# Reordering the opening of two spectral layers on one core: channel-matrix splits and cell sums moved behind the first blocks

## Chip, core and metric

The kernel runs on one NeuronCore of a Trainium2 chip. The metric is the device time of one execution in microseconds (us). The profile gives the granted TensorE clock as a share of full speed.

## What is computed

Four layers in turn on a sequence of 2048 rows of 640 numbers, all float32: attention with a dilated window of 8, a Fourier mixing layer, and both again.

```python
x = A_x
x = x + _A_ref(_layernorm(x, axis=-1), A_wqkv, A_wo)
x = x + _B_ref(_layernorm(x, axis=-1), B_dft_seq_re, B_dft_seq_im, B_dft_hid_re, B_dft_hid_im)
x = x + _A_ref(_layernorm(x, axis=-1), A_wqkv, A_wo)
x = x + _B_ref(_layernorm(x, axis=-1), B_dft_seq_re, B_dft_seq_im, B_dft_hid_re, B_dft_hid_im)
...
def _B_ref(x, dft_seq_re, dft_seq_im, dft_hid_re, dft_hid_im):
    a = jnp.einsum("bsd,ed->bse", x, dft_hid_re)
    b = jnp.einsum("bsd,ed->bse", x, dft_hid_im)
    y = jnp.einsum("ts,bse->bte", dft_seq_re, a) - jnp.einsum("ts,bse->bte", dft_seq_im, b)
    return y
```

The change lies in the two `_B_ref` layers, called spectral layers here.

## The kernel before

Each float32 operand of a matmul is split into a high and a low part (`split`, line 127: a cast on ScalarE, then a subtraction on VectorE), and each product is made of three passes (high by high, high by low, low by high).

A spectral layer (`LayerB`, line 845) first multiplies by the sequence matrix, then by the channel matrices. Its 2048 output rows are 8 tiles of 256. For a tile the sequence matrix comes in 16 blocks of 256 KB.

- Tile 0's sums `z` are accumulated in five banks (`ZTAGS`: m0, m1, xt, t0, t1) while the attention layer before it still runs.
- `run` (line 1229) then takes over. `evac` (line 980) evicts tile 0's five banks as split parts (`zt_put`, lines 973, 975, 978). `load_w` loads and splits the two channel matrices in 10 pieces of 128 rows (`split`, lines 128, 130, 132).
- The loop over the 16 blocks of tile 1 follows: `zpart` (line 950) loads a block (line 944, five buffers `win`), splits it (lines 890 and 903, two buffers) and does 15 matmuls into the same five banks (line 918).
- Tile 0's products with the channel matrices, `ymm` (line 985, matmuls on line 996), stand in that loop: one for the first 128 rows, one for the second. `yout` (line 1004) adds the residual (line 1009), stores, and in the first spectral layer computes the statistics of the next layer norm (lines 148 and 150).
- The loop also issues the cell sums. The six other tiles are computed in three pairs, each by a scheme with seven products (`pair`, line 1093), for which sums of quarters of the input are needed. `x_whole` (line 1041) makes 8 sums of high and low parts, `x_combine` makes 20 sums or differences of cells (line 1049), splits them (lines 1050 and 1051, two buffers `stg`) and stores 512 KB each (line 1052). `pair` loads them back (line 1058) with its own blocks (line 1068), which it combines (line 1114) and splits (lines 1078, 1079) ahead of its matmuls (line 1085).
- At the end of `run` tile 1's banks are evicted; the first pair uses the same banks.

The layer norm of the last quarter of the rows (lines 868, 880, 881) ends just ahead of `run`. In `run` only TensorE's order is written by hand (`manual_schedule(engines={nc.tensor.engine})`); the framework's scheduler places the instructions of VectorE, ScalarE, GpSimd and the DMA queue on SyncE, each of which is then worked off in order.

The loop before:

```python
self.evac(0)
self.load_w()
...
for s in range(NST):
    self.zpart(1, s, s + 1)
    if s == 3:
        self.ymm(0, 0, 0, KD)
        self.yout(0, 0, nstats)
    if s == 13:
        self.ymm(0, 1, 0, 2)
    if s > 1:
        for fn, args in todo[:3]:
            fn(*args)
        todo = todo[3:]
```

Of the kernel before, what the change touches and what calls it, by code (L numbers as in the profile page):

```python
# [20 lines left out]
D = 640  # L21
# [15 lines left out]
LEAD0 = (-7, -6, -5, -4, -3, -2, -1, 0, 1, 1, 2, 3, 3, 4, 5, 5)  # L37


THIN = ((20, 24, 26, 28, 32, 36, 40, 44), (12, 16, 20, 24, 28, 32, 36, 44, 48))  # L40
OUTP = (((20, 24, 28, 32), (36, 40, 44, 46)), ((20, 24, 28, 32), (36, 40, 44, 46)))
LNS = ((40, 52), (40, 52))


LEAD2 = (-7, -6, -5, -4, -2, 0, 0, 1, 1, 2, 3, 4, 4, 6, 6, 7)
ZTHIRDS = (
# [4 lines left out]
)  # L51
# [3 lines left out]
NWIN = 5  # L55
# [19 lines left out]
def tile_layers(ctx: ExitStack, tc: tile.TileContext, x, wqkv, wo, cs, wre, wim, out):  # L75
# [21 lines left out]
    nc.vector.memset(warm, 0.0)  # L97
    nc.scalar.activation(warm, warm, AF.Exp)
    T([P, 8], "pad0")
# [34 lines left out]
    class Stats:  # L134
        def __init__(self):
# [30 lines left out]
        def var_eps(self, j):  # L166
            nc.scalar.activation(self.rstd[:, j : j + 1], self.var[:, j : j + 1], AF.Copy, bias=EPS, scale=1.0 / D)  # L167

        def finish(self, j0=0, j1=4):
            r = self.rstd[:, j0:j1]  # L170
# [19 lines left out]
    def load_x(src, j, tag="xa"):  # L190
        xt = T([P, D], tag, bufs={"xa": 2}.get(tag, 1))
        nc.sync.dma_start(xt, src[:, j, :])
        return xt
# [45 lines left out]
    def layer_a(li, stats, handoff, prev):  # L239
        xin, xout = xs[li], xs[li + 1]  # L240
        first = li == 0
        ly = li // 2
        nstats = [None] * NC
# [7 lines left out]
        win = {}  # L251
        lgs = {}
# [18 lines left out]
        def x_stats(c, j, fast=False):  # L271
            if j == 0:
                stats[c] = Stats()
# [88 lines left out]
        def qkv_evac(g, cqj):  # L362
            c, q, j = cqj
            if j % 2 == 0:
                sgs[q] = T([P, 6, 2, FE], "stg", bufs=2)
# [21 lines left out]
        def q_load(u):  # L387
            c, e = u // NE, half(u, 0)[0]
            src = qb[c][e // 2]
            qs[u] = T([P, NJ, FE], "qs")  # L390
# [34 lines left out]
        def qk_mul(u, jp):  # L425
# [4 lines left out]
            nc.gpsimd.tensor_tensor(pv[:, :, 0:10], pv[:, :, 0:10], pv[:, :, 10:20], op=ALU.add)  # L430
            prq[(u, jp)] = pv

        def qk_red(u, jp):
            if jp == 0:
# [3 lines left out]
                prq.pop((u, jp))[:, :, 0:10],  # L438
# [75 lines left out]
        def wo_add(c, j, e0=0, e1=2):  # L514
            for e in range(e0, e1):
                if e == 0 and j == 0:
                    nstats[c] = Stats()
# [27 lines left out]
        def wq_split(q, k):  # L545
            split(wq[q][:, 0, k], wq[q][:, 1, k], wq[(q, k)], eng=nc.gpsimd if k % 2 else None)
# [23 lines left out]
        def early():  # L570
# [8 lines left out]
            def xt(j, part):  # L579
# [3 lines left out]

            prev.pair(
                NPAIR - 1,
                stats,
                {
                    2: lambda: (x_get(0), x_get(1)),
                    4: lambda: xt(0, 0),
                    5: lambda: (xt(0, 1), x_get(2)),  # L590
                    6: lambda: xt(1, 0),
                    7: lambda: (w0(), xt(1, 1), x_get(3)),
                    ("y", 1): lambda: xt(2, 0),
                    ("y", 2): lambda: xt(2, 1),
                    "end": lambda: (xt(3, 0), xt(3, 1)),
                },
# [11 lines left out]
        def prologue_first():  # L608
            wq_begin(0)
            for j, (k0, k1) in enumerate(((0, 3), (3, 5))):  # L610
                if j:
                    T([P, 16], "pad2")
# [47 lines left out]
            for i in range(KD):  # L660
                at(LEAD0[0] + 1 + i // 2, "misc", wq_split, 1, i)
                at(LEAD0[0] + 3 + i, "misc", wq_split, 2, i)
                at(LEAD0[0] + 5 + i, "misc", wq_split, 3, i)

        if not first:
# [10 lines left out]
        for k in range(KD):  # L676
# [7 lines left out]
        order += [  # L684
            (c, 2 * qh + i, 2 * jh + j)
            for c in range(1, NC)
            for qh in range(2)
            for jh in range(2)
            for i in range(2)
            for j in range(2)  # L690
        ]
        gs = list(LEAD0 if first else LEAD2)
        tx = {(0, j): -8 for j in range(NJ)}
        st = 4
        while len(gs) < NGRP:
            if st % 2 == 0 and len(tx) < NC * NJ:
                c, j = divmod(len(tx), NJ)
                used = [i for i, x in enumerate(order) if x[0] == c - 1 and x[2] == j]
                if used[-1] < len(gs) and gs[used[-1]] < st:
                    tx[(c, j)] = st  # L700
            cap = 0 if st < 6 else 2 if st % 2 == 0 and st not in THIN[ly] else 1
            for _ in range(max(0, cap - gs[:16].count(st))):
                if len(gs) < NGRP and len(gs) <= 16 + st and tx.get(order[len(gs)][::2], st) < st:
                    gs.append(st)
            st += 1
# [28 lines left out]
        for c in range(1, NC):  # L734
            for j in range(NJ):
                b = tx[(c, j)]
                at(b - 4, "dma", x_load, c, j)
                if first:
                    at(b - 3, "actl", x_stats, c, j)
                    at(b - 2, "fin", x_fin, c, j)  # L740
# [3 lines left out]
        for c in range(2):  # L744
            for j in range(NJ):
                a = OUTP[ly][c][j]
                tp(a, "o", c, j, 0, 2, "t1", 0, "s0" if (c, j) == (1, 3) else "ot")
                tp(a, "o", c, j, 2, 5, "t0")
                at(a + 1, "dmar", r_load, c, j, "xa" if (c, j) == (1, 3) else "xr")
# [569 lines left out]
```

## Time and profile before

| | us |
|---|---|
| runs | 1800.17, 1804.51, 1807.22 |
| median | 1804.51 |
| profiled execution | 1801.87 |
| its span, first to last instruction | 1800.0 |
| first spectral layer's opening, tile 1's blocks to the first pair | about 404 to 492 |
| the same in the second spectral layer | about 1295 to 1383 |

Rows of the timeline give start, duration, engine, line, operation and tiles, then in brackets the idle time of the engine ahead of the first instruction and what ended it. `PE` is TensorE's matmuls, `DVE` VectorE, `ACT` ScalarE, `SPq` the queue that issues DMAs. `out<-in` names tiles.

### The profile page before, as it was taken

What the parts mean: (1) busy time and instruction counts of PE and PEld (TensorE: products, weight loads), DVE (VectorE), ACT (ScalarE), POOL (GpSimd) and SP (SyncE); (2) the same over time, 40 slices, a digit from 0 to 9 for tenths busy, and PEclk for the clock granted to TensorE, in tenths of its full rate; (3) what the DMA queues carried; (4) which work ended last, traced back from release to release, by engine and by line L of the source; (5) the groups of instructions that cost most, each with busy time, mean ns of one, the idle gap of its engine ahead of it and who ended that gap; (6) DMA issues with size and microseconds to landing.
All of it is one profiled execution on the core that took longest, in us unless ns stands there. A gap on an engine that the chain in (4) does not pass through costs nothing.

```text
span 1800.0 us, 26493 instructions
## 1 busy us (share of the span) xinstructions
PE 1735.3 (96%) x8798; PEld 1506.4 (84%) x8798; DVE 1391.0 (77%) x2135; ACT 818.6 (45%) x1708; POOL 633.5 (35%) x591
## 2 busy tenths in 40 slices
PE   9999997989999999999999999998899999999999
PEld 6889896877788888888888899987787888888888
DVE  5899899987767767768739988899777676677673
ACT  5544644544445445445533334444434443443441
POOL 3799898960000000000008987889400000000000
PEclk9999999999999999999999999999999999999999
DMA  6776667648787887888737856687687876876861
GB/s 232 225 264 205 212 206 250 216 147 293 255 264 256 284 271 251 290 270 268 246 124 223 284 183 199 201 300 260 218 283 258 265 237 219 267 230 228 265 211 53
DMA packets 273994, 423.59 MB, mean 235 GB/s; under 512 B 22688, under 2 KB 153248, under 8 KB 273600
## 3 DMA queue, kind: packets, MB, share of 16 engines
q1 hardware_dynamic: 270656, 419.92, 71.7%
q10 hardware_dynamic: 3200, 1.97, 0.4%
q8 instruction: 70, 1.15, 0.3%
q14 instruction: 68, 0.56, 0.1%
HBM read 336.66 MB, written 85.14 MB: 234 GB/s over the span
## 4 chain that ended last, share of the span: by engine, by line
PE 63%; DVE 14%; DMA 11%; POOL 6%; ACT 3%; issue 2%; SPq 0%; DVEq 0%; ACTq 0%; POOLq 0%
PE m L359 16%; PE aux L996 12%; PE t L1085 9%; PE m L1085 9%; PE pq L1085 5%; PE xt L1085 4%; DMA xc<-stg 4%; PE aux L506 4%; DVE pr L428 2%; DMA win<-cs_in 2%; DVE pr L466 2%; POOL pr L481 2%; POOL pr L430 1%; POOL r L868 1%; DMA xa<-cs_in 1%
## 5 line engine op out<-in xcount | busy, mean ns | idle before, releaser
L359 PE MATMUL m<-r,s 128*128 128x480 f32 x1920 | 438.9, 383 | 6.2 <-ACT s L229 3.8
L359 PEld LDWEIGHTS m<-r,s 128*128 128x128 f32 x1920 | 358.1, 190 | 60.8 <-ACT s L229 5.5
L1078 ACT CAST r<-win 128x512 fp32r<-128x512 f32 x251 | 152.9, 620 | 175.3 <-DVE win L1114 86.9
L171 POOL TENSOR_TENSOR stats<-stats,mhalf 128x1 f32<-128x1 f32 (+1 forms) x40 | 29.1, 727 | 565.8 <-ACT stats L167 565.7
L996 PE MATMUL aux<-r2a,zo 128*128 128x320 f32 x768 | 226.0, 309 | 0.0
L481 POOL TENSOR_TENSOR pr<-pr 128x640 f32<-128x640 f32 x126 | 204.5, 1623 | 41.9 <-DVE pr L466 41.5
L428 DVE TENSOR_TENSOR pr<-pq,win 128x1280 f32<-128x1280 f32 x128 | 189.8, 1483 | 26.9 <-ACT pq L401 24.6
L996 PE MATMUL aux<-pr,zo 128*128 128x320 f32 x704 | 207.8, 309 | 0.0
L1079 DVE TENSOR_TENSOR r<-win,r 128x512 fp32r<-128x512 f32 x251 | 168.9, 687 | 45.7 <-ACT r L1078 43.5
L466 DVE TENSOR_TENSOR pr<-pq,win 128x1280 f32<-128x1280 f32 x128 | 190.8, 1491 | 4.5 <-DVE pq L461 0.2
L430 POOL TENSOR_TENSOR pr<-pr 128x640 f32<-128x640 f32 x128 | 183.5, 1434 | 19.8 <-DVE pr L428 17.0
L1085 PE MATMUL m<-r,r 128*128 128x512 f32 x594 | 151.7, 390 | 0.8 <-DVE r L1079 0.5
L996 PEld LDWEIGHTS aux<-r2a,zo 128*128 128x128 f32 x768 | 144.1, 188 | 1.9
L918 PE MATMUL m<-s,r 128*128 128x512 f32 x384 | 120.3, 401 | 18.1 <-DMA s<-c0b 7.1
L996 PEld LDWEIGHTS aux<-pr,zo 128*128 128x128 f32 x704 | 132.2, 188 | 2.0
L1085 PE MATMUL t<-r,r 128*128 128x512 f32 x495 | 132.6, 390 | 0.0
L1085 PEld LDWEIGHTS m<-r,r 128*128 128x128 f32 x594 | 111.2, 188 | 24.8 <-DVE r L1079 1.1
L918 PE MATMUL t<-s,r 128*128 128x512 f32 x384 | 117.4, 394 | 2.4 <-DVE ot L978 2.4
L482 POOL TENSOR_TENSOR pr<-pr 128x320 f32<-128x320 f32 x126 | 114.5, 909 | 9.9
L366 ACT COPY stg<-m 128x480 f32<-128x480 f32 x128 | 70.9, 556 | 100.4 <-PE m L359 88.1
L436 DVE TENSOR_REDUCE lg<-pr 128x64 f32<-128x640 f32 x128 | 104.0, 813 | 11.2 <-POOL pr L430 11.1
L1085 PEld LDWEIGHTS t<-r,r 128*128 128x128 f32 x495 | 92.9, 188 | 19.9
(270 smaller groups left out, 3231.8 us busy)
## 6 DMA issues: line engine op xcount, KB each, us to landing
win<-cs_in SPq DMA_DIRECT2D x358, 256.0 KB, 4.3
r<-xc SPq DMA_DIRECT2D x240, 256.0 KB, 4.5
win<-kvb SPq DMA_DIRECT2D x96, 440.0 KB, 4.7
xa<-cs_in SPq DMA_DIRECT2D x124, 256.0 KB, 4.3
win<-kvb SPq DMA_DIRECT2D x64, 360.0 KB, 5.1
xc<-stg SPq DMA_DIRECT2D x40, 512.0 KB, 3.7
kvb<-stg SPq DMA_DIRECT2D x60, 320.0 KB, 3.9
xr<-xs SPq DMA_DIRECT2D x40, 320.0 KB, 3.2
```

Source lines behind the costliest of these rows:

```text
L359: nc.tensor.matmul(mt[g][:, : 3 * F], st[:, a, k], wq[q][:, b, k], start=n == 0, stop=n == 14)
L428: nc.vector.tensor_tensor(pr, q, wview(u, jp, 0, [[1, FE]]), op=ALU.mult)
L430: nc.gpsimd.tensor_tensor(pv[:, :, 0:10], pv[:, :, 0:10], pv[:, :, 10:20], op=ALU.add)
L436: nc.vector.tensor_reduce(lgs[u][:, 2 * jp : 2 * jp + 2].rearrange("p j w h -> p (j w h)"), prq.pop((u, jp))[:, :, 0:10], axis=AX.X, op=AL ...
L466: nc.vector.tensor_tensor(pr.rearrange("p j w (h d) -> p j w h d", d=DH), lgs[u][:, 2 * jp : 2 * jp + 2].unsqueeze(4).to_broadcast([P, 2, ...
L481: g.tensor_tensor(pr[:, :, 0:4], pr[:, :, 0:4], pr[:, :, 4:8], op=ALU.add)
L482: g.tensor_tensor(pr[:, :, 0:2], pr[:, :, 0:2], pr[:, :, 2:4], op=ALU.add)
L918: self.last = nc.tensor.matmul(self.z[t][k], self.xn[c][:, a, j, k * P : (k + 1) * P], self.ct[s][:, b], start=s == 0 and i == 0, stop=s = ...
L996: self.last = nc.tensor.matmul(self.ym[e][:, :320], zt[(k, a, ri)][:, j2 * P : (j2 + 1) * P], w[:, e * 320 : (e + 1) * 320], start=(k, a, ...
L1078: nc.scalar.copy(hi, raw)
L1079: nc.vector.tensor_tensor(lo, raw, hi.bitcast(F32), op=ALU.subtract)
L1085: nc.tensor.matmul(bank, w(a, kb), hl[b], start=start and (a, b) == (0, 0), stop=stop and (a, b) == (1, 0),)
```

## The change

Most of the diff moves constants into a table `CFG` and reads them from there; the values that the attention layers get are those they had. In `run` the table's entries are the same for both spectral layers: `pre` is 0 for every block, `post` says how many items of the list `todo` follow each block, `y` after which block each fifth of tile 0's two products comes.

```diff
+ 'run': [{'pre': [0, 0, 0, 0, 0, 0, 0, 0, 0, 0, 0, 0, 0, 0, 0, 0],
+          'post': [0, 4, 4, 4, 3, 3, 3, 3, 3, 3, 3, 3, 3, 3, 3, 3],
+          'y': [[6, 6, 6, 6, 6], [13, 13, 16, 16, 16]]},
...
+    eps = T([P, 1], "eps")
+    nc.vector.memset(eps, EPS)
+    nc.scalar.add_instruction(
+        mybir.InstLoadActFuncSet(name=nc.get_next_instruction_name(), ins=[], outs=[], act_func_set_id=6)
+    )
     nc.scalar.activation(warm, warm, AF.Exp)
-    T([P, 8], "pad0")
...
-        def load_w(self):
-            self.wr = T([P, 2, KD, D], "r2a", F32R)
-            self.wi = []
-            for k in range(KD):
-                raw = load_x(wre, k)
-                split(self.wr[:, 0, k], self.wr[:, 1, k], raw)
-                raw = load_x(wim, k)
...
+        def load_w(self, i):
+            k = i // 2
+            if i == 0:
+                self.wr = T([P, 2, KD, D], "r2a", F32R)
+                self.wi = []
+            if i % 2 == 0:
+                split(self.wr[:, 0, k], self.wr[:, 1, k], load_x(wre, k))
+            else:
+                wt = T([P, 2, D], f"pr{k}" if k < 4 else "zo3", F32R)
+                split(wt[:, 0], wt[:, 1], load_x(wim, k), neg=True)
+                self.wi.append((wt[:, 0], wt[:, 1]))
...
         def run(self, nstats):
+            R = CFG["run"][self.li // 2]
             self.evac(0)
-            self.load_w()
             todo = []
             for i in range(0, NP, 2):
                 todo += [(self.x_whole, (side, i)) for side in (2, 0)]
                 todo += [(self.x_combine, (m, i)) for m in XC]
+            todo = [(self.load_w, (i,)) for i in range(2 * KD)] + todo
             with tc.manual_schedule(engines={nc.tensor.engine}):
                 for s in range(NST):
+                    for _ in range(R["pre"][s]):
+                        fn, args = todo.pop(0)
+                        fn(*args)
                     self.zpart(1, s, s + 1)
-                    if s == 3:
-                        self.ymm(0, 0, 0, KD)
-                        self.yout(0, 0, nstats)
-                    if s == 13:
-                        self.ymm(0, 1, 0, 2)
-                    if s > 1:
-                        for fn, args in todo[:3]:
-                            fn(*args)
-                        todo = todo[3:]
+                    for h in range(2):
+                        ks = [k for k in range(KD) if R["y"][h][k] == s]
+                        if ks:
+                            self.ymm(0, h, ks[0], ks[-1] + 1)
+                        if 4 in ks:
+                            self.yout(0, h, nstats)
+                    for _ in range(R["post"][s]):
+                        if todo:
+                            fn, args = todo.pop(0)
+                            fn(*args)
```

So the code calls the 10 pieces of the channel matrices and the 28 cell-sum items behind blocks 1 to 12, and tile 0's first product comes behind block 6 in place of block 3. The number of matmuls and of DMAs is the same. The order of instructions in the two built programs:

- TensorE: the 60 matmuls of tile 0's first product stand behind block 6 in place of block 3, in both spectral layers; all else as before.
- GpSimd: as before.
- VectorE, ScalarE and the DMA queue: as before but for one memset at the start and a stretch in each spectral layer that begins with block 6. VectorE there, around the product's additions (line numbers of before; L1049 and L1051 belong to a cell sum, L903 to a block, L1041 to `x_whole`):

```
before, from block 6 to block 9:
  L1009 L1051 L1009 L1049 L1051 L903(6) L1049 L1051 L1049 L903(7) L1041 L1051 L1049 L903(8) L1041 L1051 L1049 L903(9)
after, from block 6 to block 9:
  L903(6) L1041 L1051 L130 L1049 L903(7) L1051 L903(8) L1049 L1051 L1049 L1051 L1049 L1009 L1041 L1051 L1009 L1049 L1041 L1051 L1049 L903(9)
before, around tile 1's eviction:
  L1049 L975 L1051 L1079 L1114 L1079 L1079 L978 L978 L975 L978 L1009 L1114 L1009 L978 L975
after, around tile 1's eviction:
  L1049 L975 L1079 L1051 L1114 L1079 L1049 L978 L978 L975 L1051 L1079 L1009 L978 L1009 L978 L975 L1079 L1114 L1114
```

More of the change, by code (lines that the diff above doesn't have):

```diff
@@ L54 @@
 STG = (-1, "dma2")
-NWIN = 5
+NWIN = CFG['nwin']
 ZTAGS = ("m0", "m1", "xt", "t0", "t1")
@@ L251, in layer_a @@
         win = {}
+        whole = {divmod(x, 2) for x in C["whole"]}
         lgs = {}
@@ L586, in early @@
                 stats,
[L587 to L596, printed above, removed]
+                {keys[h]: (lambda v=v: [fn(*args) for fn, args in v]) for h, v in hooks.items()},
             )
@@ L683, in layer_a @@
         order = [(0, q, j) for q in range(NQ) for j in range(NJ)]
[L684 to L705, printed above, removed]
+        for c in range(1, NC):
+            order += [(c, x // 2, 2 * (x % 2) + j) for x in C["ord"][c - 1] for j in range(2)]
+        gs = C["gs"]
+        tx = {(c, j): C["tx"][4 * c - 4 + j] for c in range(1, NC) for j in range(NJ)}
         for g, cqj in enumerate(order):
@@ L815, in layer_a @@
             nc.vector.tensor_copy(mk, mask)
-            for s in range(LEAD0[0], last + 1):
-                for ph in PHASES:
+            for s in range(gs[0], last + 1):
+                for ph in C["ph"][s >= 48].split():
                     for fn, args in plan.pop((s, ph), ()):
@@ L1173, in pair @@
                     self.product(f1, self.x_plain(*k2(i), 512), p21, False, i == NP - 1)
-                es = store("stg", 2)
+                es = store("stg", CFG["bufs"]["stg"])
                 for b in range(2):
```

182 lines of the change are left out of this document (120 added, 62 removed), and 13 rows, old and new, of tables (CFG, ZTHIRDS).

## Prediction

> **What bounds the kernel now.** I read the page's busy table first, then the waits of TensorE in the two stretches that the change touches (the opening of each spectral layer), then a table of those stretches, then the timeline around the waits.
>
> ```profile
> PE 1735.3 (96%) x8798; PEld 1506.4 (84%) x8798; DVE 1391.0 (77%) x2135; ACT 818.6 (45%) x1708; POOL 633.5 (35%) x591
> ...
> 404.00:492.00 88.00, 81.46 (x389) 67.41 (x390) 68.46 (x106) 40.01 (x73) 0.00 (x0) 1.00 0.79 274
> 1295.00:1383.00 88.00, 81.64 (x392) 67.99 (x393) 69.24 (x107) 37.51 (x66) 0.00 (x0) 1.00 0.81 275
> ```
>
> The columns of the two stretches are length, busy time of TensorE, its weight loads, VectorE, ScalarE and GpSimd, then the granted clock, the DMA share and GB/s. TensorE is the bound: 96% overall, 81.5 of 88 us in each stretch at full clock. VectorE (68.5 us) and the DMA engines (0.79) are the runners-up. So only a wait of TensorE can be won, and any delay that reaches TensorE is lost.
>
> ```profile
> PE t L1085 <- DVE ot L978: 1.9, 1, 1.9
> PE m L918 <- DVE zo L975: 1.2, 1, 1.2
> PE m L918 <- DVE r L868: 1.0, 1, 1.0
> PE t L918 <- DVE ot L978: 0.9, 1, 0.9
> PE m L918 <- ACT r L880: 0.7, 1, 0.7
> PE m L918 <- DVE s L903: 0.4, 1, 0.4
> PE xt L918 <- DVE zo L975: 0.3, 1, 0.3
> PE aux L996 <- DVE zo L130: 0.3, 1, 0.3
> ...
> PE t L1085 <- DVE ot L978: 1.8, 1, 1.8
> PE t L918 <- DVE ot L978: 1.5, 1, 1.5
> PE m L918 <- DVE zo L975: 0.9, 1, 0.9
> PE m L918 <- ACT r L880: 0.7, 1, 0.7
> PE aux L996 <- DVE zo L130: 0.7, 1, 0.7
> PE m L918 <- DVE r L868: 0.6, 1, 0.6
> PE m L918 <- DVE s L903: 0.4, 1, 0.4
> ```
>
> These are all waits of TensorE there (us in total, times, longest), first spectral layer above, second below: 6.7 and 6.6 us. This is everything that a reordering of these stretches can win by itself, some 13 us of 1800.
>
> **The change, part by part.** Its words promise an earlier opening, so I first ask which of these waits it can reach.
>
> *The opening itself.* L868 and L880 are the layer norm of the last quarter, which ends ahead of the change. L975 and L978 under L918 are the eviction of tile 0, whose banks tile 1 needs. In the order of the two programs VectorE, ScalarE and the DMA queue hold the same rows in the same sequence from the layer norm through this eviction up to the 7th block: the scheduler had already pulled two block splits and the eviction in between the matrix splits, whatever order the code called them in. I cost this at 0. What the title names is then worth nothing, and the hidden work (8 remaining matrix splits) stays where it was.
>
> *The moved product.* What does move on TensorE is one product of tile 0 (L996, 60 matmuls), from behind block 3 to behind block 6.
>
> ```profile
> 426.16 0.30 PE L996 MATMUL aux<-r2a,zo 128*128 128x320 f32 x1
> ...
> 435.84 0.63 PE L918 MATMUL m<-s,r 128*128 128x512 f32 x2
> ...
> 446.06 0.62 PE L918 MATMUL m<-s,r 128*128 128x512 f32 x2
> ```
>
> It ran from 426.16 to 435.84, and the three blocks after it (4, 5, 6) to 446.06, so 3.41 us a block. They swap places. The product's last fifth waited for the last matrix split (L130 on L996: 0.3 and 0.7 us); it now comes 10.2 us later, so this wait goes: -1.0 us for both layers. Blocks 4 and 5 stand at their old places in VectorE's order; block 6 moves ahead of the product's two additions (L1009). Nothing is late there, I cost it at 0. If that cover failed, the next bound is the 0.4 us that L918 already waits for L903 once in each layer.
>
> *The end of the stage.* The largest wait, 1.9 and 1.8 us, is a bank of tile 1 that the first pair's products need.
>
> ```profile
> 486.65 1.55 PE L1085 MATMUL m<-r,r 128*128 128x512 f32 x6
> 488.04 0.84 PE L1085 MATMUL xt<-r 128*128 128x512 f32 x3
> 490.79 0.93 PE L1085 MATMUL t<-r 128*128 128x512 f32 x3 [1.91 <-DVE ot L978]
> ...
> 486.89 0.41 DVE L978 TENSOR_TENSOR zo<-t,zo 128x256 fp32r<-128x256 f32 x1
> 487.22 0.48 DVE L1009 TENSOR_TENSOR xr<-aux,xr 128x320 f32<-128x320 f32 x1
> 489.21 0.69 DVE L1114 TENSOR_TENSOR win<-xa,win 128x512 f32<-128x512 f32 x1 [1.51 <-DMA xa<-cs_in]
> 489.82 0.48 DVE L1009 TENSOR_TENSOR xr<-aux,xr 128x320 f32<-128x320 f32 x1
> 490.23 0.41 DVE L978 TENSOR_TENSOR ot<-t,zo 128x256 fp32r<-128x256 f32 x1
> ```
>
> TensorE could have taken bank t at 488.04 plus 3 matmuls of 0.23 (six took 1.39), so 488.7. VectorE stood before L1114 for a DMA until 489.21, and the second L1009 and the last L978 are queued behind it. In the new order L1114 stands behind the whole eviction, so what is left is L1009, L978, L1009, L978. Against that, the last cell sums come later. A cell sum is L1049, a cast, L1051 and a store, in two buffers:
>
> ```profile
> 472.09 0.69 DVE L1049 TENSOR_TENSOR stg<-s 128x512 f32<-128x512 f32 x1 [1.10 <-DMA xc<-stg]
> ...
> 474.51 0.68 DVE L903 TENSOR_TENSOR s<-win,s 128x512 fp32r<-128x512 f32 x1
> 474.61 0.33 SPq L1052 DMA_DIRECT2D xc<-stg  x1
> ...
> 478.86 0.69 DVE L1049 TENSOR_TENSOR stg<-s,s 128x512 f32<-128x512 f32 x1 [0.51 <-DMA xc<-stg]
> ...
> L1051 DVE TENSOR_TENSOR stg<-stg 128x512 fp32r<-128x512 f32 x20 | 13.7, 687 | 3.4 <-ACT stg L1050 2.8
> L1041 DVE TENSOR_TENSOR s<-r 128x1024 f32<-128x1024 f32 x8 | 9.7, 1218 | 0.1
> ```
>
> From one L1049 to the next in the same buffer are 478.86 - 472.09 = 6.8 us. In the new order the 16th of 20 sums takes the place of the 17th, behind block 14 at about 470.9, so the 20th starts two buffer turns later, at 484.5, between the evictions. Behind it VectorE has its own 0.69, two L978, an eviction, L1051 and one more split before the first L1009: 484.5 + 0.69 + 0.66 + 3 x 0.6 = 487.6, and bank t is free after L1009, L978, L1009, L978 at 489.2. The wait shrinks from 1.9 to about 0.5, a saving of 1.4. The bounds are 0 (the 20th sum a further 1.5 us late) and the whole wait of 1.9 and 1.8. I take 1.1 a layer, nearer the walk than 0: -2.2.
>
> *What can be late next.* After the moved product the queues hold more ahead of block 9 than they held ahead of block 6.
>
> ```profile
> 436.82 0.74 ACT L148 ACTIVATE junk<-xr 128x640 bf16<-128x640 f32 x1 [1.16 <-DVE xr L1009]
> 437.69 0.83 ACT L150 ACTIVATE junk<-xr,stats 128x640 bf16<-128x640 f32 x1
> ...
> DVE stg L1049 <- DMA xc<-stg: 10.9, 9, 3.2
> ```
>
> VectorE: L1009, L1041, L1051, L1009, L1049, L1041, L1051, L1049, then block 9's L903. From 446.1 the second L1009 ends at 446.1 + 0.48 + 1.22 + 0.6 + 0.48 = 448.9. ScalarE then runs the two statistics passes with a cast of a sum between (0.9 + 0.6 + 1.0) and casts block 9 by 452.1. TensorE has blocks 7 and 8 (6.8 us, to 452.9) and needs the low half of 9 a third of a block later, at 454.0. VectorE's second L1049 waits for the store of a sum whose L1051 ended at 448.5; issued by 448.6 and landed 4.25 us later (474.61 to 478.86) it frees the buffer at 452.9, and L1049 and L903 end at 454.2: 0.2 late. I take +0.3 a layer, +0.6; the ends are 0 and the longest store wait of the stage, 3.2 a layer.
>
> By the Trainium skill (DMA: Bandwidth & Descriptors, "Anatomy of one DMA") a transfer takes 2.0 us and its bytes over 436 GB/s, 3.2 us for a 512 KB store; the trace has 4.25 at this load. By that rule of the skill block 9 would be in time and the sum 0.6 lower.
>
> *Rest.* One memset of 128x1 on VectorE ahead of the first load (at most a 0.48 us L1009, hidden behind the loads); one activation table load as before, with another set number, for a ScalarE that is idle more than half the time: 0. The rest of the diff turns constants into a table of the same values; TensorE's and GpSimd's order elsewhere is unchanged.
>
> *Sum.* -1.0 - 2.2 + 0.6 = **-2.6 us**. The profiled execution took 1801.87 us (span 1800.0 and 1.87 around it), so 1799.3 for that execution. It lies 2.64 below the median of the three runs, 1804.51, which gives **1801.9 us** as the median to expect.
>
> **Rivals.**
> - *The opening does move* (the title is right and the order's sameness misleads). The eviction waits go: 1.2 + 0.3 + 0.9 in the first layer, 0.9 + 1.5 in the second, 4.8 us more, 1797.1. For it: they are the second largest waits. Against: the rows stand in the same sequence, and the splits that precede the eviction wait for the same DMAs.
> - *The end stays as it is.* The 20th sum's store decides instead of L1114's DMA: -1.0 + 0.6, 1804.1. For it: 9 L1049 waited 10.9 us for stores in this stretch. Against: L1114 did stand in the way for 1.51 us and doesn't any more.
> - *Slower: the store ahead of block 9.* If the second L1049 meets the longest store wait, TensorE stops 3.2 us after block 8 in both layers: +6.4 - 1.0 - 2.2 = +3.2, 1807.7. It decides from 1.6 us a layer on. For it: block 9's slack by the walk is nil. Against: nine such waits average 1.2 us. It can cost more through the clock:
>
> ```profile
> 994.41 0.50 PE L332 MATMUL xt<-s,nident 128*128 128x512 f32 x1 [1.81 <-ACT s L328]
> ...
> 994.80:998.20 3.40, 3.40 (x11) 2.85 (x10) 3.23 (x6) 0.92 (x3) 3.24 (x5) 0.50 0.99 374
> ```
>
> After a wait of 1.81 us TensorE ran 3.4 us at a clock of 0.50, which loses 1.7 us. With two such the rival stands at 1811.1. Such stretches also come and go with the phase of a run, so I count 1.7 us either way as noise.
>
> The Trainium skill (TensorE: Matmul & The Clock Gate, "HAM oscillation") asks for idle gaps above about 3.4 us before the clock halves; the row shows that 1.81 can be enough. By that rule of the skill alone a 3.2 us wait would stay at full clock, 1807.7.
>
> **How the numbers follow.** Forecast 0.58, opening moves 0.06, end stays 0.22, slower 0.14. From the forecast the bounds of its own terms reach -5.5 (the whole end wait, 3.7, and the L903 waits, 0.8) to about +3; the three runs spread from 4.3 below to 2.7 above their median. Half of that spread with the bounds gives 1796 to 1807.5, which takes in the other cases but for the tail of the slower one. A difference of 0.5% is 9 us, about what a measurement of this kernel can tell from no change. No case but the slower one with both clock losses and a bad spread, or the opening with all else won, comes near it: faster 0.03, same 0.94, slower 0.03.
>
> **What would show it.** L996 no longer waits for L130's line; the wait for L978 at the first pair falls under 1 us; the opening's waits for the layer norm and the eviction stay within some tenths; block 9 waits at most 0.5 us. I am wrong if the opening's 4.1 and 3.7 us change by more than 1 us, or a wait above 1.5 us appears behind the moved product.

## The result and the profile after

| | before | after |
|---|---|---|
| median, us | 1803.55 (22 runs) | 1800.62 (22 runs) |
| lowest to highest, us | 1799.49 to 1810.14 | 1795.64 to 1805.08 |
| ratio of the times, 95% interval | | 0.998 (0.997 to 0.9989) |
| profiled execution, us (its span) | 1801.87 (1800.0) | 1805.08 (1803.2) |

The kernel after is 0.2% faster there, with an interval that leaves out 1. Two later comparisons of the same two kernels gave 0.9991 (0.9975 to 1.0006) and 0.9999 (0.9986 to 1.0011), so the gain is 0 to 0.2%, at most some 3 us.

The profiled execution of after is the slowest of its 22 runs, 3.2 us longer than that of before. Only its stages can be set beside those of before. First the table of the two stretches (columns as in the prediction):

```profile
404.00:492.00 88.00, 81.67 (x392) 67.33 (x391) 68.75 (x106) 40.70 (x74) 0.08 (x1) 1.00 0.78 272
1298.00:1386.00 88.00, 81.99 (x398) 68.81 (x397) 69.10 (x106) 38.52 (x67) 0.54 (x1) 1.00 0.79 274
```

TensorE's busy time in 88 us went from 81.46 and 81.64 to 81.67 and 81.99: the same work and, as far as stretches that are not cut at the same matmuls can tell, a little less waiting. TensorE's waits, first layer above, second below:

```profile
PE t L1128 <- DVE ot L1021: 1.6, 1, 1.6
PE m L965 <- DVE s L950: 1.0, 1, 1.0
PE m L965 <- DVE r L915: 1.0, 1, 1.0
PE t L965 <- DVE ot L1021: 0.9, 1, 0.9
...
PE m L965 <- DVE zo L1018: 1.6, 1, 1.6
PE t L965 <- DVE ot L1021: 1.5, 1, 1.5
PE t L1128 <- DVE ot L1021: 1.1, 1, 1.1
```

(L1128 was L1085, L965 was L918, L1021 was L978, L1018 was L975, L950 was L903, L915 was L868, L1039 was L996; further down L1084 was L1041, L1092 to L1094 were L1049 to L1051, L1052 was L1009, L1157 was L1114, L937 was L890, L188 to L192 were L128 to L132.) The product's wait for a matrix split is gone from both lists. The opening's waits for L915, L1018 and L1021 are there as before. So is the largest one of the first layer, the first pair's for bank t; it is 1.6 and 1.1 where it was 1.9 and 1.8, not under 1 us as forecast. A new one of 1.0 stands amid the blocks. The timeline of after in the first layer, rows of VectorE and TensorE in order of time:

```profile
405.13 1.22 DVE L1084 TENSOR_TENSOR s<-r 128x1024 f32<-128x1024 f32 x1
405.42 0.73 PE L965 MATMUL m<-s,r 128*128 128x512 f32 x2 [0.69 <-ACT r L927]
406.27 0.82 DVE L915 TENSOR_TENSOR r<-win,r 128x640 fp32r<-128x640 f32 x1
407.14 1.19 PE L965 MATMUL m<-s,r 128*128 128x512 f32 x4 [0.99 <-DVE r L915]
...
412.60 1.21 DVE L1084 TENSOR_TENSOR s<-r 128x1024 f32<-128x1024 f32 x1
...
414.63 1.63 PE L965 MATMUL t<-s,r 128*128 128x512 f32 x6 [0.93 <-DVE ot L1021]
...
466.98 1.28 DVE L1157 TENSOR_TENSOR win<-xa,win 128x512 f32<-128x512 f32 x2
468.19 0.68 DVE L950 TENSOR_TENSOR s<-win,s 128x512 fp32r<-128x512 f32 x1
468.92 0.74 PE L965 MATMUL m<-s,r 128*128 128x512 f32 x2 [1.03 <-DVE s L950]
...
486.44 0.69 DVE L1092 TENSOR_TENSOR stg<-s 128x512 f32<-128x512 f32 x1 [0.71 <-DMA xc<-stg]
486.98 1.90 PE L1128 MATMUL m<-r,r 128*128 128x512 f32 x6
...
488.31 0.68 DVE L1094 TENSOR_TENSOR stg<-stg 128x512 fp32r<-128x512 f32 x1
488.71 0.85 PE L1128 MATMUL xt<-r 128*128 128x512 f32 x3
488.91 0.68 DVE L1122 TENSOR_TENSOR s<-xa,s 128x512 fp32r<-128x512 f32 x1
489.51 0.48 DVE L1052 TENSOR_TENSOR xr<-aux,xr 128x320 f32<-128x320 f32 x1
...
490.64 0.41 DVE L1021 TENSOR_TENSOR ot<-t,zo 128x256 fp32r<-128x256 f32 x1
...
491.20 0.93 PE L1128 MATMUL t<-r 128*128 128x512 f32 x3 [1.64 <-DVE ot L1021]
```

Three things are to be seen. In the opening a sum of a whole quarter (L1084) stands ahead of the last layer norm (L915) and another amid the eviction, as before. Block 13's split (468.19) stands behind two combinations for the first pair (466.98), and TensorE waits 1.03 us for it. At the end the 20th cell sum waits for a store until 486.44, and bank t is free 4.6 us later, behind VectorE's own work.

A list of waits shows only the longer gaps. For a sharper measure I took from the trace, in each of the two stages, every distance from one matmul's start to the next, less the usual one (0.227 us at 512 columns, 0.147 at 320), and added these up by place. The stretch has 393 matmuls, from the last 15 of tile 0 (the first of them is the anchor, at 404.44 in before and in the row at 405.42 in after) to the 18th of the first pair. *Opening* reaches to the end of block 0, *product* is tile 0's two products, *end* the first pair. A stretch at half clock counts as a wait here.

| us, first and second layer | opening | blocks | product | end | length |
|---|---|---|---|---|---|
| before | 4.70, 4.02 | 1.22, 1.32 | 0.86, 0.90 | 2.20, 2.13 | 88.27, 87.67 |
| after | 3.88, 4.81 | 2.26, 0.82 | 0.0, 0.0 | 2.26, 1.39 | 87.68, 86.30 |

The two stages are 0.59 and 1.37 us shorter, 1.96 together. The rest of the span (all but the two stages) was 1624.1 us in before and 1629.2 in after, though every engine's order there is the same but for one memset and some places early in the first pair. Over the twelve further profiles below it lies between 1622.2 and 1628.5; the two with the highest mean granted clock (0.994) have 1622.2 and 1623.8, that of after has 0.990. A step from 0.994 to 0.990 is some 7 us of 1800 by estimate, as much as lies between 1622.2 and 1629.2; but the profile with the product's move alone has 0.990 too, and 1624.1, so the clock is not the whole of it. This scatter is larger than the change.

### The profile page after: what moved, and what is told of

Its sections match the earlier page's. It is cut to its first block, busy times and chain, and to the rows that moved or that the text cites. A ratio compares the mean times of both kernels' runs of the same rounds, so it can differ in the third digit from the quotient of the medians.

```text
span 1803.2 us, 26504 instructions
## 1 busy us (share of the span) xinstructions
PE 1739.4 (96%) x8798; PEld 1508.4 (84%) x8798; DVE 1390.6 (77%) x2136; ACT 818.9 (45%) x1708; POOL 633.4 (35%) x591
## 3 DMA queue, kind: packets, MB, share of 16 engines
q10 hardware_dynamic: 3200, 1.97, 0.4%
## 4 chain that ended last, share of the span: by engine, by line
PE 64%; DVE 14%; DMA 10%; POOL 6%; issue 3%; ACT 3%; SPq 1%; DVEq 0%; ACTq 0%; POOLq 0%
PE m L429 17%; PE aux L1039 12%; PE t L1128 9%; PE m L1128 9%; PE pq L1128 5%; PE xt L1128 5%; PE aux L577 4%; DMA xc<-stg 3%; DVE pr L498 2%; DMA win<-cs_in 2%; POOL pr L552 2%; DVE pr L537 2%; POOL pr L501 1%; POOL r L915 1%; DVE r L1122 1%
## 5 line engine op out<-in xcount | busy, mean ns | idle before, releaser
L1039 PE MATMUL aux<-r2a,zo 128*128 128x320 f32 x768 | 226.1, 309 | 0.0
L1039 PE MATMUL aux<-pr,zo 128*128 128x320 f32 x704 | 207.8, 309 | 0.0
L1128 PE MATMUL m<-r,r 128*128 128x512 f32 x594 | 152.1, 390 | 1.1 <-DVE r L1122 0.5
L1039 PEld LDWEIGHTS aux<-r2a,zo 128*128 128x128 f32 x768 | 144.3, 188 | 2.0
L965 PE MATMUL m<-s,r 128*128 128x512 f32 x384 | 120.6, 401 | 18.9 <-DMA s<-c0b 9.2
L1039 PEld LDWEIGHTS aux<-pr,zo 128*128 128x128 f32 x704 | 132.3, 188 | 2.1
L1128 PE MATMUL t<-r,r 128*128 128x512 f32 x495 | 132.6, 390 | 0.0
L1128 PEld LDWEIGHTS m<-r,r 128*128 128x128 f32 x594 | 111.0, 188 | 25.6 <-ACT r L1121 1.2
L965 PE MATMUL t<-s,r 128*128 128x512 f32 x384 | 117.5, 394 | 2.4 <-DVE ot L1021 2.4
L1128 PEld LDWEIGHTS t<-r,r 128*128 128x128 f32 x495 | 92.9, 188 | 20.0
```

What stands on the lines that cost most here:

```text
L965: self.last = nc.tensor.matmul(self.z[t][k], self.xn[c][:, a, j, k * P : (k + 1) * P], self.ct[s][:, b], start=s == 0 and i == 0, stop=s = ...
L1039: self.last = nc.tensor.matmul(self.ym[e][:, :320], zt[(k, a, ri)][:, j2 * P : (j2 + 1) * P], w[:, e * 320 : (e + 1) * 320], start=(k, a, ...
L1128: nc.tensor.matmul(bank, w(a, kb), hl[b], start=start and (a, b) == (0, 0), stop=stop and (a, b) == (1, 0),)
```

## The experiments

Twelve runs follow, each timed in five rounds beside the kernel before: nine other kernels, one of them twice, and the changed kernel twice more.

**The product's move alone.** The kernel before with one edit:

```diff
-                    if s == 3:
+                    if s == 6:
                         self.ymm(0, 0, 0, KD)
                         self.yout(0, 0, nstats)
```

> The kernel before with one edit: tile 0's first product stands behind block 6 instead of block 3. On every engine its instructions then stand in the order of the changed kernel, but for the one memset. Theory (the product's move is the whole change): the ratio to before is that of the changed kernel, 0.998 (0.997 to 0.999); the product's own waits, 0.86 and 0.90 us in the two layers, fall below 0.1, and the stages get 0.6 to 1.4 us shorter each. Rival (the new order of the calls, the memset or the other activation table set carry a part): the ratio lies nearer 1.000 than 0.998.

Measured: 1.000 (0.9991 to 1.0009). Opening 3.96 and 3.85, blocks 1.97 and 0.25, product 0.0, end 1.96 and 2.24, lengths 87.16 and 85.61. VectorE and TensorE work in the order of after, but for the one memset, and the stages lie among those of after: the move is the whole change. In the time it was not to be seen in this comparison: the expected 0.998 was missed. This interval and that of the first comparison (0.997 to 0.9989) do not meet, for two kernels with the same order; so an interval tells of its own comparison only, and a difference of 0.1 to 0.2% needs more than one.

**The order of the calls alone.** The changed kernel with the product back in its place:

```diff
-          'post': [0, 4, 4, 4, 3, 3, ...], 'y': [[6, 6, 6, 6, 6], ...
+          'post': [0, 4, 6, 3, 3, 3, ...], 'y': [[3, 3, 3, 3, 3], ...
```

> The changed kernel with the first product put back behind block 3; the calls still begin with the second tile's blocks, and the matrix splits and cell sums follow as list items. Theory (the scheduler's order is the old one whatever the order of the calls): ratio to before 1.000, within 0.1%; the product waits 0.8 to 0.9 us in each layer again, and the first pair waits about 2 us for its bank behind the late block's DMA. Rival (the order of the calls is worth something by itself): 0.998 to 0.999.

Measured: 0.9997 (0.9986 to 1.0009). Opening 4.22 and 4.06, blocks 0.02 and 0.33, product 1.26 and 0.51, end 1.87 and 2.13, lengths 86.66 and 86.31. TensorE's waits of this kernel, first layer above, second below:

```profile
PE t L1128 <- DVE ot L1021: 1.6, 1, 1.6
...
PE aux L1039 <- ACT zo L188: 0.4, 1, 0.4
PE aux L1039 <- DVE zo L190: 0.3, 1, 0.3
...
PE t L1128 <- DVE ot L1021: 1.8, 1, 1.8
...
PE aux L1039 <- DVE zo L190: 0.3, 1, 0.3
```

The product waits again, for the last matrix split's cast and subtraction. The new order of the calls, the memset and the other table set are worth nothing that can be measured here, where the interval is some 0.1% to either side. And the stages of this kernel, in the order of before, differ from those of before by 1.6 and 1.4 us: so far do two profiles of one order lie apart.

**Behind block 4.**

```diff
-          'y': [[6, 6, 6, 6, 6], [13, 13, 16, 16, 16]]
+          'y': [[4, 4, 4, 4, 4], [13, 13, 16, 16, 16]]
```

> The changed kernel with the first product behind block 4, one block later than before and two earlier than in the change. Theory (the product gained because its operands, the last matrix splits, came up to 0.9 us late, and one block of 3.4 us covers that): the product's waits are below 0.1 us here too, -1.8 us over both layers, and what differs from the changed kernel lies in the blocks and the end only; ratio to before 0.998 to 0.9995. Rival (the gain is in the blocks and cell sums that the product was moved past): the product's waits go, but waits of the same size come back between blocks 5 and 15, ratio 1.000.

Measured: 1.0019 (1.0009 to 1.0029). Product 0.0 in both layers, so one block is cover enough for the last split. Opening 3.32 and 4.72, blocks 0.04 and 1.52, end 2.85 and 1.81, lengths 85.49 and 87.32: stages as short as the change's, yet the time is above before, outside what either theory expected. Its one profile does not show where these 3.4 us (0.0019 of 1799.54) are; this stays open.

**The whole sums on GpSimd.** All 8 sums of whole quarters a layer, the two L1084 of the opening among them, off VectorE's queue:

```diff
-            nc.vector.tensor_tensor(self.whole[side], v[:, 0], v[:, 1], op=ALU.add)
+            nc.gpsimd.tensor_tensor(self.whole[side], v[:, 0], v[:, 1], op=ALU.add)
```

> The changed kernel with the 8 sums of whole quarters (128x1024, 1.22 us each on VectorE) on GpSimd, which has nothing to do in these stages. Theory (in the opening VectorE's queue delays TensorE: such a sum stands ahead of the last layer norm and another amid the eviction): the opening's waits fall from 3.9 and 4.8 us by about 1 us for each of the two sums, 2 to 3 us over both layers or more, and the time by 0.1 to 0.2%. Rival (the opening waits for DMAs and for ScalarE, and the sums only fill the gap): the waits keep their size under other names, ratio to the changed kernel 1.000. A third way: a sum takes 2.4 us on GpSimd (worked out from its 1.57 us for 128x640), its reader comes later, and the first cell sums, stores and the end of the stage move back: slower by 0.5 to 2 us.

Measured: 1.0129 (1.0116 to 1.0142), 23 us slower. Opening 4.03 and 4.34, blocks 7.84 and 6.52, end 5.02 and 4.84, lengths 96.17 and 94.97, some 18 us more than with the change. The third way had the sign, at a tenth of the size. The timeline of this kernel, GpSimd (`POOL`) and VectorE:

```profile
403.85 2.62 POOL L1084 TENSOR_TENSOR s<-r 128x1024 f32<-128x1024 f32 x1 [0.72 <-PE t L965]
404.44 2.72 DVE L915 TENSOR_TENSOR r<-win,r 128x640 fp32r<-128x640 f32 x1 [0.19 <-ACT r L927]
...
412.13 2.41 POOL L1084 TENSOR_TENSOR s<-r 128x1024 f32<-128x1024 f32 x1 [5.66 <-PE t L965]
412.71 0.69 DVE L1018 TENSOR_TENSOR ot<-t,ot 128x512 fp32r<-128x512 f32 x1
...
425.14 2.71 POOL L1084 TENSOR_TENSOR s<-r 128x1024 f32<-128x1024 f32 x1 [10.60 <-DVE stg L1092]
425.72 2.68 DVE L1094 TENSOR_TENSOR stg<-stg 128x512 fp32r<-128x512 f32 x1
```

L915 takes 0.82 us in after and 2.72 here; it begins 0.59 us into GpSimd's sum and ends 0.7 behind the end of it. L1094 takes 0.68 in after and 2.68 here. Both read two tiles in SBUF. L1018, which reads a bank and one tile, took its usual 0.69 us amid a GpSimd sum (412.71). So it goes through both layers: 7 and 8 operations with two tiles in SBUF begin amid one of the 8 sums, and each ends behind it, which costs VectorE some 13 us a layer; the 8 sums had taken 9.8 there (8 x 1.22). The opening's L915 came later and not sooner. That the blocks and the end lost by the other ones, L1094 above all, fits but was not followed row by row. The Trainium skill (SBUF — State Buffer, "SBUF: two separate sides") says that GpSimd and a VectorE operation with two inputs in SBUF exclude each other for a whole instruction; the rows agree, that of L1018 too.

**The changed kernel again**, on another chip, unedited.

> The changed kernel again, beside runs of the kernel before on another chip. In the first four experiments two kernels whose VectorE, ScalarE, TensorE and DMA orders are those of the change and of the kernel before differed by nothing: 1.000 and 0.9997. Theory (the true difference is the sum of the stages' waits, product -1.8, blocks about +1, opening and end about 0, so -0.5 to -1.5 us): ratio 0.9992 to 1.000. Rival (the changed kernel has something that the moved product alone has not, by the place of its tiles in memory or the table set): 0.998 again. The product's waits are below 0.1 us, and the bank's wait at the first pair is 1 to 2 us, in both cases.

Measured: 0.9991 (0.9975 to 1.0006). Opening 4.12 and 3.96, blocks 1.10 and 0.12, product 0.0, end 2.43 and 1.91, lengths 86.93 and 85.27. The interval holds the theory's 0.9992 to 1.000 and the rival's 0.998, so this run does not decide between them.

**VectorE and ScalarE in written order.** The opening as the title has it, by taking the two engines' order from the scheduler:

```diff
-            self.evac(0)
+            with tc.manual_schedule(engines={nc.vector.engine, nc.scalar.engine}):
+                self.evac(0)
...
-            with tc.manual_schedule(engines={nc.tensor.engine}):
+            with tc.manual_schedule(engines={nc.tensor.engine, nc.vector.engine, nc.scalar.engine}):
...
-          'post': [0, 4, 4, 4, 3, 3, 3, 3, ...
+          'post': [0, 4, 4, 4, 3, 3, 2, 2, ...
```

> The changed kernel with VectorE's and ScalarE's order in the spectral opening written by hand too: both work off the loop as it is called, so the eviction of tile 0 really stands ahead of the sums of whole quarters and of most matrix splits, and all 20 cell sums end before the eviction of tile 1; the list is spread as 4, 4, 4, 3, 3, then 2 items a block. Theory (what the title names would be worth the eviction's waits if the scheduler did it): the opening's waits fall from about 4.2 to 1.5 to 2.5 us, those at the first pair from 2 to below 0.7, together about 3.5 us a layer, and the time by 0.2 to 0.4%. Rival (VectorE then stands idle behind each cast of ScalarE, 0.7 us for each of 20 sums, and behind the stores, with the next block's split queued behind it): TensorE waits 3 us or more between blocks 5 and 15 of each layer, and the ratio is 1.000 or more.

Measured: 1.0386 (1.0367 to 1.0405). Opening 2.43 and 2.72, blocks 33.45 and 33.25, end 6.82 and 1.89. The opening came near what was expected (1.5 to 2.5), the end did not (below 0.7), and the rival's place, the blocks, was right at ten times its price. TensorE's waits for ScalarE's cast of a block in the first layer, one of these waits with the cast that ScalarE had ahead of that block's, and VectorE's timeline of this kernel:

```profile
PE m L965 <- ACT s L937: 19.7, 8, 4.2
```

```profile
423.51 0.74 ACT L188 ACTIVATE pr<-xa 128x640 fp32r<-128x640 f32 x1 [1.04 <-DMA xa<-wim_in]
...
424.81 1.22 PE L965 MATMUL m<-s,r 128*128 128x512 f32 x2 [4.24 <-ACT s L937]
```

```profile
444.80 0.69 DVE L1092 TENSOR_TENSOR stg<-s 128x512 f32<-128x512 f32 x1 [2.88 <-DMA xc<-stg]
...
447.96 0.69 DVE L950 TENSOR_TENSOR s<-win,s 128x512 fp32r<-128x512 f32 x1
459.99 0.49 DVE L1052 TENSOR_TENSOR xr<-aux,xr 128x320 f32<-128x320 f32 x1 [11.34 <-PE aux L1039]
```

In written order a block's cast stands behind whatever was called ahead of it. At 424.81 that is a matrix piece's cast, which waited for its DMA. Behind block 6 it is the product's additions: VectorE waits 11.34 us for TensorE, ScalarE's statistics wait for VectorE, and the next block's cast is queued behind them, 3.7 us of TensorE (at 464.50). The scheduler had put work in between. Part of the loss is the clock, whose mean over the two stages is 0.89 and 0.91 instead of 1.00; by estimate that is up to 13 and 11 us of their 122 and 117. The other waits were not followed.

**Tile 1's eviction ahead of the last additions.**

```diff
-                    self.yout(0, 1, nstats)
                 self.evac(1)
+                self.yout(0, 1, nstats)
```

> The changed kernel with tile 1's eviction called ahead of the additions of tile 0's second product. On VectorE one addition (128x320, 0.48 us) then stands behind the eviction of bank t instead of ahead of it; else two neighbours change places. Theory (the first pair's wait for bank t is the length of VectorE's queue behind the last cell sum): the wait of 1.3 to 1.8 us falls by 0.3 to 0.5 in each layer, 0.6 to 1.0 us in all, 0.03 to 0.05% of the time and not to be seen in it, only in the trace. Rival (the wait is set by ScalarE's evictions or by the product that still runs): the wait keeps its size.

Measured: 0.9986 (0.9975 to 0.9996), like the changed kernel beside it (0.9991). The longest gap of the end, for bank t, is 1.8 in seven of the eight stages with the change's order and 1.42 and 1.41 here, so the theory's 0.3 to 0.5 came true at this place: VectorE's queue sets this wait. The whole end shows nothing of it: 2.52 and 2.01, where the change's order has 1.39 to 2.56. The first pair's earlier gap for bank m was 0.64 in the first layer, against up to 0.55 with the change's order; whether the wait moved there is not shown.

**Two stores for each cell sum.**

```diff
-            nc.sync.dma_start(self.xc[m][:, i : i + 2], hl.bitcast(F32))
+            for a in range(2):
+                nc.sync.dma_start(self.xc[m][:, i : i + 2, a], hl[:, :, a].bitcast(F32))
```

> The changed kernel with each cell sum stored as two transfers of 256 KB instead of one of 512 KB. Theory (the cell sums go at the pace of the stores, two buffers in 6.8 us, and the 20th sum sets the end of the stage): the first pair's wait follows the time of a store; with two transfers side by side it lands up to 1 us sooner than 4.25 us and VectorE's waits for stores (10 to 12 us in a layer) fall by a third, the end by 0.5 us or more; if a transfer is bound by the bytes at the engines' load of 0.8, it lands at the same time and nothing changes, within 0.5 us in each stage. Rival (the pace is VectorE's and ScalarE's own work): VectorE's waits for stores change and the end does not.

Measured: 1.0002 (0.999 to 1.0015). Opening 3.31 and 3.80, blocks 3.28 and 3.53, end 0.78 and 0.89, lengths 86.63 and 87.50. The row of the DMA issues, first of after, then of this kernel (size, median us from issue to landing):

```profile
xc<-stg SPq DMA_DIRECT2D x40, 512.0 KB, 4.6
```

```profile
xc<-stg SPq DMA_DIRECT2D x80, 256.0 KB, 3.2
```

And VectorE's timeline of this kernel in the first layer, whose anchor is at 407.20 (that of after is at 405.42):

```profile
484.74 0.69 DVE L1092 TENSOR_TENSOR stg<-s 128x512 f32<-128x512 f32 x1
...
491.35 0.42 DVE L1021 TENSOR_TENSOR ot<-t,zo 128x256 fp32r<-128x256 f32 x1
```

The store lands 1.4 us sooner, and the 20th sum comes at 77.5 us behind the anchor instead of 81.0. The end falls by 1.3 us a layer, so the sums do set it. But in the first layer bank t is free only 1.1 us sooner (84.6 behind the anchor instead of 85.6), and the rest of the fall there is that TensorE comes to the pair 0.4 us later (82.0 instead of 81.6): 7.0 us of VectorE's other work now stand between the two where it was 4.6. And VectorE's sums, which come sooner, stand ahead of block splits: the blocks lose 2.5 us a layer, and TensorE's waits for L950 are 1.6 and 2.4 where they were 1.0 and 0.5. What is won at one place is paid at another.

**The opening held, the rest left to the scheduler.** Eviction first, then two matrix splits, then two whole sums, in written order; all else as in the change:

```diff
-            self.evac(0)
...
+            with tc.manual_schedule(engines={nc.vector.engine, nc.scalar.engine}):
+                self.evac(0)
+                for n in (0, 0, 8, 8):
+                    fn, args = todo.pop(n)
+                    fn(*args)
...
-          'post': [0, 4, 4, 4, 3, 3, ...
+          'post': [0, 2, 2, 4, 3, 3, ...
```

> The changed kernel with VectorE's and ScalarE's order fixed by hand for the opening alone: eviction of tile 0, then the first two matrix splits, then the first two sums of whole quarters; everything behind is left to the scheduler. On VectorE neither splits nor sums then stand ahead of the last layer norm or amid the eviction. The cell sums come later: the 18th to 20th stand amid the eviction of tile 1. Theory (the opening is worth some 1.5 us a layer, as where both engines' whole loop was in written order and it fell from 4.2 to 2.4 and 2.7, and whatever delays the cell sums is paid back at the end): opening 2.0 to 2.8, the first pair's wait for its bank 3 to 8 us instead of 1.5, the stage no shorter, ratio to before 1.000 to 1.005. Rival (the opening's gain stays): the end grows by less than 1 us, the stage is 1 to 2 us shorter and the ratio 0.997 or below.

Measured: 0.9973 (0.9961 to 0.9985), 1795.42 us. Opening 1.13 and 1.60, blocks 4.00 and 0.71, product 0.0, end 1.40 and 2.09, lengths 85.82 and 83.67. The rival was right: the end did not grow, and the ratio came within 0.0003 of its 0.997. The timeline of this kernel in the first layer, VectorE, ScalarE and TensorE:

```profile
406.61 0.83 DVE L915 TENSOR_TENSOR r<-win,r 128x640 fp32r<-128x640 f32 x1 [0.18 <-ACT r L927]
...
411.49 0.68 DVE L1018 TENSOR_TENSOR zo<-xt,zo 128x512 fp32r<-128x512 f32 x1
412.09 0.41 DVE L1021 TENSOR_TENSOR zo<-t,zo 128x256 fp32r<-128x256 f32 x1
...
414.82 2.35 DVE L1084 TENSOR_TENSOR s<-r 128x1024 f32<-128x1024 f32 x2
...
457.66 0.69 DVE L1092 TENSOR_TENSOR stg<-s,s 128x512 f32<-128x512 f32 x1 [2.53 <-DMA xc<-stg]
...
458.43 0.62 ACT L1093 CAST stg<-stg 128x512 fp32r<-128x512 f32 x1 [5.11 <-DVE stg L1092]
458.95 1.13 ACT L937 CAST s<-win 128x512 fp32r<-128x512 f32 x2
...
459.62 0.73 PE L965 MATMUL m<-s,r 128*128 128x512 f32 x2 [2.00 <-ACT s L937]
```

No whole sum stands ahead of L915 or amid the eviction; both follow at 414.82. At block 11 the store frees a buffer late, L1092 waits 2.53 us, ScalarE's cast of that sum waits for L1092, and block 11's cast is queued behind it: 2.00 us of TensorE. That is the mechanism of the prediction's slower rival, at another block. The clock behind that wait, from the table of stretches:

```profile
460.60:464.00 3.40, 3.40 (x10) 2.65 (x10) 2.50 (x4) 1.02 (x2) 0.00 (x0) 0.56 0.79 260
```

**The same with two stores.**

> The kernel with the fixed opening, and each cell sum stored as two transfers of 256 KB as well, which brought the first pair's wait down from about 2 to 0.8 us and cost 2 to 3 us of waits amid the blocks. Theory (the sums' pace, set by stores and two buffers, hands the delay on from place to place): opening 2.0 to 2.8; the end shorter by 1 us or more than with whole stores; blocks 3 us or more; ratio to before 0.999 to 1.004. Rival (the two gains add, and the blocks hold): ratio 0.997 or below.

Measured: 1.0053 (1.0036 to 1.0069), above the theory's range too. Opening 1.27 and 1.87, blocks 6.60 and 2.01, end 4.99 and 3.40, lengths 92.41 and 86.56. The gains do not add; the end grew where the theory had it shrink. Why it grew stays open.

**The change and the held opening side by side**, on one chip.

> The changed kernel, on the same chip as the next kernel, so that the two are set against the same runs of the kernel before. By the two ratios so far, 0.998 and 0.9991, 0.998 to 0.9995 here.

> The kernel with the opening fixed by hand, again. Theory (its opening's 5.4 us are kept, as the first run's stages showed, and the changed kernel's gain is the product's 1.8 us less what the blocks give back): ratio to before 0.996 to 0.998, and 0.1 to 0.2% below the changed kernel beside it. Rival (the two differ by chip only): ratios within 0.05% of each other.

Measured: the change 0.9999 (0.9986 to 1.0011), 1798.24 us; the held opening 0.9982 (0.9969 to 0.9996), 1795.86 us. Both ratios are just above what was expected; the first interval leaves out the first comparison's 0.998. In the change: opening 3.81 and 4.70, blocks 0.67 and 0.08, end 2.56 and 2.51, lengths 86.32 and 86.56. In the other: opening 0.74 and 1.90, blocks 2.37 and 1.35, end 2.19 and 2.50, lengths 84.57 and 85.03. Its median is 2.4 us below the change's and 3.2 below before. The two intervals overlap; the lengths of the stages, layer by layer, in two profiles of the one and four of the other, do not.

Means a layer over all profiles with the same order of instructions in these stages:

| us a layer | opening | blocks | product | end | length |
|---|---|---|---|---|---|
| order of before (2 profiles) | 4.25 | 0.72 | 0.88 | 2.08 | 87.23 |
| order of after (4 profiles) | 4.14 | 0.91 | 0.0 | 2.16 | 86.48 |
| opening held (2 profiles) | 1.34 | 2.11 | 0.0 | 2.05 | 84.77 |

## Why the prediction was right in the time, and where its steps were not

The forecast of -2.6 us, and its 1801.9, agree with the first comparison (1800.62; -2.9 by the medians). By the last table the change is worth 2 x (87.23 - 86.48) = 1.5 us, and two profiles of one order differ by up to 1.6 us in the length of one layer. That the sum came out so near is in part luck: it has 2.2 us at the end that did not come and 0.8 us too little for the product, and the first comparison shows more than the two later ones.

- *The opening, costed at 0:* right. It went from 4.25 to 4.14 a layer, the order of the instructions there is the same, and the kernel with the new call order alone shows 0.9997. The bound "by more than 1 us" held by layer: 4.70 to 3.88, 4.02 to 4.81.
- *The moved product, -1.0:* the mechanism was right, the size too small. It measured -1.8 (0.88 a layer to 0.0). I read the term off the list of waits, which had 0.3 and 0.7; the smaller gaps that it leaves out held the rest.
- *The end of the stage, -2.2:* this step failed. No gain was measured (2.08 to 2.16 a layer), and the rival "the end stays as it is" was right at this place. L1157 no longer stands in the eviction's way, as the prediction said. But its walk put the 20th sum at 484.5, that is 80.1 us behind the anchor of before (404.44), and it came at 81.0, waiting for a store. So bank t, which VectorE's chain frees, came free 0.6 us sooner (490.64 - 404.44 = 86.2 behind the anchor before, 491.05 - 405.42 = 85.6 after) and not the 1.4 of the walk. And the walk held TensorE's arrival fixed: TensorE came to the pair 0.65 sooner (486.65 - 404.44 against 486.98 - 405.42), so the wait kept its size. The two-store kernel showed that the end follows the sums. One thing that the sum of waits hides: in all 16 layers of eight profiles (the orders of before and after, the product behind block 4, the two stores) the pair's 18th matmul starts 2.0 to 2.1 us behind the release of bank t. The stage is as long as VectorE's chain to that release, and a wait won ahead of it counts only as far as the chain ends sooner.
- *Block 9, +0.6:* the size was near, which is luck, for the place was wrong. The blocks cost 0.19 more a layer, 0.4 in all, where single layers of one order range from 0.1 to 2.3. Block 9 did not wait; in the first layer block 13 did, by 0.9 to 1.2 in three of the four profiles, behind combinations for the first pair. The store time of the Trainium skill that the prediction sets beside its 4.25 us (DMA: Bandwidth & Descriptors, "Anatomy of one DMA", 3.2 us) is in that section a fit for DMAs of the GpSimd path; these stores go through SyncE's queue, and their median in after is 4.6 us.
- *The rest at 0:* the kernels with and without the memset, the table set and the list differ by 0.0003, less than the interval of some 0.1% to either side can tell.
- *The rival "the opening does move":* it did not, but its price was real. With the order held, the opening's waits fell by 2.8 a layer, 5.6 in all where 4.8 was forecast; 2.4 of it came back in the blocks, and 3.4 us stayed (2 x (86.48 - 84.77)).
- *The slower rival:* its mechanism exists, as the held opening's block 11 shows, but needs cell sums in another place.

## What to carry to other kernels

Where a framework's scheduler places the instructions, the order of the calls is a wish: read the order that each engine got, and where it matters, fix just that stretch by hand and leave the rest to the scheduler. A stage that ends with a queue on another engine pays a gain ahead of it back as a wait there, unless that queue gets shorter too. Price a wait by the distances between the bounding engine's instructions and not by the list of its longest waits, and take several profiles of one order before believing a microsecond.

## What the runs showed of the hardware that was not expected

- *GpSimd holds VectorE up, but not in every operation:* 2.72 us for an L915 of 0.82, with two tiles in SBUF; 0.69 as always for an L1018 that reads a bank. An idle engine is no free place for an addition when VectorE works on pairs of tiles meanwhile.
- *Half clock after short waits, and not always.* In the kernel with the held opening a wait of 2.00 us was followed by 3.4 us at a mean clock of 0.56. Its second run had the same wait, 2.06 us, and full clock behind it:

```profile
456.79 0.73 PE L965 MATMUL m<-s,r 128*128 128x512 f32 x2 [2.06 <-ACT s L937]
```

```profile
456.90:460.30 3.40, 3.40 (x15) 2.81 (x16) 2.27 (x5) 0.98 (x2) 0.00 (x0) 1.00 0.74 261
```

In the kernel with the product's move alone, waits of 0.69 and 0.98 us, 1.7 us apart in the opening, were followed by it; the second one and the stretch behind it:

```profile
406.22 1.34 PE L918 MATMUL m<-s,r 128*128 128x512 f32 x4 [0.98 <-DVE r L868]
```

```profile
407.20:410.60 3.40, 3.40 (x9) 2.62 (x9) 2.65 (x7) 2.70 (x7) 0.00 (x0) 0.51 1.02 376
```

The Trainium skill (TensorE: Matmul & The Clock Gate, "HAM oscillation") asks for idle gaps above about 3.4 us. Neither 2.00 nor 0.98 is one, and the clock halved; the measurement decides. What else it takes these runs do not show: the openings of before and after have the same two waits (0.69 and 0.99 in the rows of after), at full clock. With the product's move alone the loss was hidden, since TensorE would have waited for the eviction: that layer's opening lost 3.96 us in all, less than the 4.25 that is usual.
